# Batch 0's attention by halves of the heads, batch 1's turns by transfers, and batch 2's loads straight behind w_out

## The chip, the cores and the metric

The kernel runs on one core of one Trainium2 chip. The time is the device time of that core in microseconds (us), the median of several executions. The engines of the core work side by side and wait for one another by semaphores: TensorE (PE in the profile; its weight loads are the row PEld), VectorE (DVE), ScalarE (ACT) and GpSimd (POOL). SyncE (SP) only issues transfers. Transfers issued from SP and ACT go to queues that the profile names hardware_dynamic (q1 for SP), those from POOL to q0, software_dynamic. All of them are carried out by the same 16 DMA engines. GpSimd's queue can convert f32 to bf16 on the way.

## The reference

Two layers in a row: attention with a cosine weighting and no softmax, and a feed-forward layer with squared ReLU. There are 8 batches, 8 heads, 576 positions, 64 numbers per head; 4608 tokens of 512 numbers, and 2048 hidden units.

```python
r = np.maximum(x, 0.0)                              # for q and for k
phi = np.concatenate([r * c, r * s], axis=-1)       # c, s: cos and sin of the position
kv = np.einsum('bhsf,bhsd->bhfd', k_p, v)           # per head 128 x 64
z = np.sum(k_p, axis=2)                             # per head 128
num = np.einsum('bhsf,bhfd->bhsd', q_p, kv)
den = np.einsum('bhsf,bhf->bhs', q_p, z)[..., None] + 1e-06
x = (num / den)                                     # then tokens x (heads * 64)
h = x @ w_in
r = np.maximum(h, 0.0)
g = r * r
out = g @ w_out
```

## The kernel before, in words

**Tiling.** The 576 positions of a batch are four blocks of 128 (j = 0 to 3) and a tail of 64 (j = J = 4), which packs four heads over two halves of the partitions. Per block, `declare_feature` makes the cosine and the sine half of phi (a ReLU times a column, on ACT or DVE), `declare_v` casts v to bf16 beside a column of ones, and `declare_kz` multiplies k_p with v over the five blocks into two PSUM banks, so that kv and z come together. `declare_num` multiplies q_p with kv and z and then divides on DVE (three instructions), which gives x. Two turns (transposes) are needed: q_p must have its features on the partitions before `declare_num`, and x its channels before the feed-forward layer. There are two ways to turn: on PE through a matmul with the identity and a copy out of PSUM (`declare_qT_pe`, `declare_xT_pe`), or by a transposing transfer from SP (`declare_qT`, `declare_xT`). Before the change, batches 0 and 1 take the first, batches 2 to 7 the second.

**The feed-forward layer.** `declare_plain` makes one product of two blocks of hidden units with 256 tokens (8 matmuls into one bank), a ReLU on ACT into `rt` (two buffers), and a square on DVE into `gT`; a batch of 512 main tokens has 16 of them. The first two are split into pieces of 128 tokens. `declare_rows` multiplies batch 0's gT with w_out, 64 matmuls of 512 columns. Later batches use sums and differences of blocks of the weights (`declare_w1_sums`, `declare_w2_sums`, 7 products in place of 8). w_in and w_out come in four quarters each, cast to bf16 by GpSimd's queue: `load_w1(i, 4)`, `load_w2(i, 4)`. Product number hb needs quarter hb // 4.

**The order.** `prologue()` is written out by hand: the loads of batch 0, w_in, its attention up to x of blocks 0 and 1. The rest is declared as operations with their engines, costs, reads, writes and a place (`pos`), and `Planner.plan` puts them into an order by a list schedule: on PE by slot, on the other engines by how late an operation may be. `SHIFTS` lists corrections by number of operation (`n:by`, and an engine if one is fixed). `given` declares something that the prologue does, with the time at which the planner is to take it as done; `given([("w1", i)], ...)` does this for the quarters of w_in. The planner fixes the order of the instructions alone: each engine's queue then runs in that order, and waits are for data and buffers. In particular `pos` of a load holds nothing up on the chip. A POOL transfer also waits for the eighth POOL transfer before it, since eight semaphores go round.

**Buffers.** k, v and q have one f32 buffer each. So a load of the next batch waits until the engines have read the last piece of the one before. Six PSUM banks are free to all ("F"), two are for long sums ("B").

## Time and profile before

| what | us |
|---|---|
| median of 3 runs (lowest, highest) | 279.13 (278.8, 279.6) |
| the profiled execution | 278.33 |
| its span, first to last instruction | 276.6 |
| PE busy in the span | 269.0 |
| DVE, ACT, POOL busy | 219.1, 192.6, 28.4 |

The profiled execution is 1.7 us longer than its span. Its times count from the span's start. A row of the timeline gives the start, the time from there to the end of the last of the merged instructions, the engine, the line, the operation with out<-in, and in brackets the idle time ahead with what ended it. Most operations are issued by helpers, so one line (L429 is the helper of all matmuls, L418 the square, L407 and L405 the features) stands for many tiles, and the tiles tell them apart: `xT,w1sb` is a plain product, `w2sb,gT` of 512 columns are rows, `vx,kp` is kv and z, `kvz,sums` or `kvz,qpT` is the numerator, `ident,qp` (L580) and `ident,x` (L668) are turns on PE.

### The profile page before, as it was taken

Reading aid. Unit: us, or ns where it says so; the run is one execution under the profiler, and the core shown is the slowest. Engines: PE = TensorE matmul, PEld = TensorE weight load, DVE = VectorE, ACT = ScalarE, POOL = GpSimd, SP = SyncE. Lnnn points to the kernel's source line nnn. Section 1 sums busy time; section 2 is a strip of 40 time slices with the busy share of each in tenths; the row PEclk is TensorE's granted clock in tenths of the full one; section 3 lists DMA queues with packets and bytes.
Section 4 is the critical chain, followed back from the end, with each engine's and each line's share of the span. In section 5 each row is a group of like instructions: output and inputs, shape, how many; then the busy total and the mean of one; then the engine's idle time right before and its main releaser. Section 6 shows DMA issues by size and latency. Waiting matters only on the chain.

```text
span 276.6 us, 7125 instructions
## 1 busy us (share of the span) xinstructions
PE 269.0 (97%) x2846; PEld 227.8 (82%) x2851; DVE 219.1 (79%) x515; ACT 192.6 (70%) x385; POOL 28.4 (10%) x46
## 2 busy tenths in 40 slices
PE   8979999999999999999999999999999999999994
PEld 3658856789888988888888888988988888888883
DVE  1849996998795896799977999799946997279741
ACT  3767862798798796499848995699738643685421
POOL 8925244100000000000000000000000000000000
PEclk9999999999999999999999999999999999999999
DMA  7999999776999999899899428997583301200024
GB/s 228 311 206 287 330 256 374 220 174 148 368 191 257 281 248 238 220 331 160 237 266 377 114 40 167 330 219 210 57 233 77 94 32 42 112 1 2 8 88 134
DMA packets 77824, 53.01 MB, mean 192 GB/s; under 512 B 52032, under 2 KB 73024, under 8 KB 77792
## 3 DMA queue, kind: packets, MB, share of 16 engines
q1 hardware_dynamic: 70368, 37.63, 54.7%
q0 software_dynamic: 7280, 14.81, 19.8%
q8 instruction: 22, 0.36, 0.5%
q10 hardware_dynamic: 144, 0.13, 0.1%
q14 instruction: 10, 0.08, 0.1%
HBM read 36.70 MB, written 9.44 MB: 167 GB/s over the span
## 4 chain that ended last, share of the span: by engine, by line
PE 81%; DVE 11%; DMA 2%; issue 2%; POOL 2%; ACT 1%; POOLq 0%; DVEq 0%
PE banks L429 78%; DVE gT L418 3%; DVE rs L421 3%; DVE gs L426 3%; DMA q<-in_q_dram 2%; PE banks L580 1%; DVE gTt L418 1%; PE banks L668 1%; PE banks L1132 1%; ACT qp L405 1%; POOL kt L365 1%; DVE x L628 1%; POOL vt L365 0%; ACT sums L412 0%; DVE kp L407 0%
## 5 line engine op out<-in xcount | busy, mean ns | idle before, releaser
L429 PEld LDWEIGHTS <-w1sb 128*128 128x128 bf16 x784 | 72.7, 98 | 8.7
L429 PE MATMUL banks<-xT,w1sb 128*128 128x256 bf16 (+1 forms) x576 | 68.3, 267 | 0.1
L429 PEld LDWEIGHTS <-gs 128*128 128x128 bf16 x512 | 49.5, 98 | 7.0 <-DVE gs L426 0.7
L429 PE MATMUL banks<-w2sb,gT 128*128 128x256 bf16 (+1 forms) x284 | 44.8, 295 | 0.2 <-issue 0.2
L429 PEld LDWEIGHTS <-gT 128*128 128x128 bf16 x400 | 37.4, 98 | 7.5
L415 ACT ACTIVATE rt<-banks 128x512 bf16<-128x512 f32 x64 | 37.2, 602 | 9.2 <-PE banks L429 4.5
L429 PEld LDWEIGHTS <-w1s 128*128 128x128 bf16 x320 | 30.6, 98 | 3.9 <-issue 0.2
L429 PE MATMUL banks<-w2sb,gs 128*128 128x256 bf16 x256 | 32.7, 273 | 0.1
L429 PE MATMUL banks<-w2s,gs 128*128 128x256 bf16 x256 | 32.1, 273 | 0.1
L421 DVE CUSTOM_DVE_ANT_0 rs<-banks,sums 128x512 bf16<-128x512 f32 x40 | 27.0, 684 | 3.8 <-ACT sums L829 3.1
L418 DVE TENSOR_TENSOR gT<-rs 128x1024 bf16<-128x1024 bf16 (+1 forms) x50 | 28.0, 580 | 1.2 <-ACT rs L415 0.6
L426 DVE TENSOR_TENSOR ysb<-banks,sums 128x256 f32<-128x256 f32 x32 | 13.5, 422 | 17.6 <-PE banks L429 9.4
L418 DVE TENSOR_TENSOR gT<-rt 128x512 bf16<-128x512 bf16 x48 | 19.4, 420 | 7.1 <-ACT rt L415 7.0
L415 ACT ACTIVATE rs<-banks 128x512 bf16<-128x512 f32 x40 | 23.5, 606 | 2.0 <-PE banks L429 1.8
L405 ACT ACTIVATE kp<-k,sin_col 128x512 bf16<-128x512 f32 x32 | 22.4, 725 | 0.5 <-DMA k<-in_k_dram 0.5
L429 PE MATMUL banks<-xT,w1s 128*128 128x256 bf16 x160 | 22.7, 273 | 0.0
L429 PE MATMUL banks<-xs,w1s 128*128 128x256 bf16 x160 | 22.7, 273 | 0.0
L405 ACT ACTIVATE qp<-q,sin_col 128x512 bf16<-128x512 f32 x32 | 22.0, 720 | 1.0 <-DMA q<-in_q_dram 1.0
L426 DVE TENSOR_TENSOR gs<-gT 128x1024 bf16<-128x1024 bf16 x28 | 19.2, 689 | 3.1 <-PE banks L429 2.7
L628 DVE TENSOR_TENSOR x<-banks,den 128x512 bf16<-128x512 f32 x30 | 20.7, 691 | 1.0
L429 PE MATMUL banks<-xTt,w1sb 128*128 128x256 bf16 x128 | 16.1, 273 | 0.0
L407 DVE TENSOR_SCALAR kp<-k,cos_col 128x512 bf16<-128x512 f32 x26 | 12.0, 501 | 5.0 <-DMA k<-in_k_dram 5.0
(105 smaller groups left out, 362.8 us busy)
## 6 DMA issues: line engine op xcount, KB each, us to landing
out_dram<-ysb SPq DMA_DIRECT2D x13, 512.0 KB, 3.6
k<-in_k_dram SPq DMA_DIRECT2D x6, 1024.0 KB, 6.4
v<-in_v_dram SPq DMA_DIRECT2D x5, 1024.0 KB, 7.5
q<-in_q_dram SPq DMA_DIRECT2D x5, 1024.0 KB, 9.3
v<-in_v_dram POOLq DMA_DIRECT2D x3, 1024.0 KB, 8.2
w1sb<-in_moe_w_in_dram POOLq DMA_DIRECT2D x4, 512.0 KB, 10.9
w2sb<-in_moe_w_out_dram POOLq DMA_DIRECT2D x4, 512.0 KB, 12.4
q<-in_q_dram POOLq DMA_DIRECT2D x2, 1024.0 KB, 9.1
```

The lines of the kernel that those rows point to most:

```text
L365: eng.dma_start(out=tail[g * TAIL : (g + 1) * TAIL, :, :], in_=src[b, g * HH : (g + 1) * HH, MAIN:S, :].rearrange("h p d -> p h d"),)
L405: nc.scalar.activation(out=dst, in_=src, func=ACTF.Relu, scale=col)
L407: nc.vector.tensor_scalar(out=dst, in0=src, scalar1=0.0, scalar2=col, op0=ALU.max, op1=ALU.mult)
L415: nc.scalar.activation(out=out, in_=in_, func=ACTF.Relu)
L418: nc.vector.tensor_tensor(out=out, in0=in_, in1=in_, op=ALU.mult)
L421: nc.vector._custom_dve(TENSOR_ADD_SAT, out=out, in0=in0, in1=in1, s0=float("inf"), s1=0.0)
L426: nc.vector.tensor_tensor(out=out, in0=in0, in1=in1, op=op)
L429: nc.tensor.matmul(out=out, lhsT=lhsT, rhs=rhs, start=start, stop=stop, skip_group_check=True)
L580: nc.tensor.transpose(t[:, h, :], qp_at(b, j)[:, h, :], ident[:, :])
L628: nc.vector.tensor_tensor(out=x_at(b, j).rearrange("p (b k) (l d) -> p b k l d", b=n, l=2), in0=n4[:, :, :, 0:D].rearrange("p b (k l) d -> ...
L668: nc.tensor.transpose(t[:, kb, :], x_at(b, j)[:, kb, :], ident[:, :])
L1132: nc.tensor.matmul(out=banks[:, 6 + i % 2, :], lhsT=ident[:, :], rhs=zeros, start=True, stop=True)
```

## The change

It has four parts.

1. **Batch 0's attention.** It is no longer written out in the prologue but declared (`declare_first`) and ordered by the planner with everything else. All loads of batch 0 are issued by SP: k, k's tail, q's first half, v's tail, v in two halves of the heads, q's second half, q's tail. GpSimd makes the features of k's block 3. kv and z, the copy, the numerator, the division and the turn of x of blocks 0 and 1 are done for heads 0 to 3 first and then for heads 4 to 7. w_in's loads stand on POOL behind a one-element copy that reads v's first half. Between the planned operations of the head, `fill` puts matmuls without a use on PE where the planner sees a gap.
2. **Batch 1's turns.** `declare_att` now calls `declare_qT` and `declare_xT` for batch 1 as well: three transposing transfers for q_p, three for x.
3. **Order of the POOL transfers.** It becomes w_out's first quarter, q of batch 1, second quarter, k, v, third and fourth quarter, then q, k and v of batch 2. `declare_load` gets a parameter `gate` that could hold a load until some x has been made; no call gives it.
4. **The planner's figures.** Costs, `t0`, `T1` and all of `SHIFTS` are new.

```diff
-21:4.5 31:1.0 44:-3.0 53:1.5 60:1.0 74:3.0 80:2.0 93:-7.5 105:-0.5 132:-2.5 134:2.0 146:-7.0
...
+10:-5.0 29:-12.0 33:-3.0 37:-2.5 43:-9.5:ACT 48:2.5 73:-1.5 77:-3.5 90:-21.0:ACT 109:0.5 111:5.5
...
-    def declare_load(b, nm, eng, pos=None, after=()):
+    def declare_load(b, nm, eng, pos=None, after=(), size=3.4, gate=None):
...
+                if gate and fn is load_main:
+                    nc.gpsimd.tensor_copy(out=at(buf)[0:1, 0, 0, 0:1], in_=x_at(*gate)[0:1, 0, 0:1])
                 fn(src, nm, buf.i, b, queue)
...
-            if b > 1 and (j == J or j % 2):
+            if j == J or j % 2:
                 declare_qT(b, j // 2)
-            elif b == 1:
-                declare_qT_pe(b, j, npos[j] - 3.5, DVE1)
         for j in range(NS):
             declare_num(b, j, npos[j])
-            if b > 1 and (j == J or j % 2):
+            if j == J or j % 2:
                 declare_xT(b, j // 2)
-            elif b == 1:
-                declare_xT_pe(b, j, npos[j] + 2.0, BOTH)
...
     def prologue():
+        for src, nm, part in (
+            (k, "k", 0), (k, "kt", 0), (q, "q", 0), (v, "vt", 0), (v, "v", 0), (v, "v", 1), (q, "q", 1), (q, "qt", 0)
+        ):
...
-        load_main(k, "k", 0, 0, nc.sync)
-        load_tail(k, "k", 0, 0, nc.gpsimd)
-        load_main(v, "v", 0, 0, nc.gpsimd)
-        load_tail(v, "v", 0, 0, nc.gpsimd)
         constants()
-        load_main(q, "q", 0, 0, nc.gpsimd, 2)
-        for i in range(31):
-            nc.tensor.matmul(out=banks[:, i % 2, :], lhsT=zeros[:, 0:P], rhs=zeros, start=True, stop=True)
...
+        fill(28)
+        for c, col in ((0, cos_col), (D, sin_col)):
+            nc.gpsimd.tensor_scalar(
+                out=at(kp_of(0, J - 1))[:, :, c : c + D], in0=piece("k", 0, J - 1),
+                scalar1=0.0, scalar2=col[:, J - 1 : J], op0=ALU.max, op1=ALU.mult,
+            )
+        nc.gpsimd.tensor_copy(out=w1sb[0:1, 0, 0:1], in_=mem["v"][0:1, 0, 0, 0, 0:1])
         for i in range(4):
             load_w1(i, 4)
...
+    def fill(n):
+        for _ in range(n):
+            nc.tensor.matmul(out=banks[:, SPARE, :], lhsT=zeros[:, 0:P], rhs=zeros, start=True, stop=True)
...
     for i in range(4):
-        given([("w1", i)], 12.2, size=2.6)
+        given([("w1", i)], 11.7, size=2.6)
...
+    def declare_first():
+        feature = lambda nm, j, c: declare_feature(nm, 0, j, c, BOTH)
...
+        for g in range(2):
+            hs = slice(g * HH, (g + 1) * HH)
...
+            for j in (J, *range(J)):
+
+                def kz(_, j=j, g=g):
...
+        for g in range(2):
+            den, bks = plan.buf("den"), [plan.buf("F"), plan.buf("F")]
+            for j in range(2):
+
+                def num(_, j=j, g=g, bk=bks[j]):
...
+    ORDER1 = []
+    pos = 21.0
+    for nm in "0q1kv23----QK-V":
+        if nm != "-":
+            ORDER1.append((pos, nm))
+        pos += 1.0 if nm == "-" else 2.65 if nm in "0123" else 3.1
...
-    declare_load(1, "q", "POOL", 17.0)
-    declare_w2_load(0, 19.0, 10.0)
-    declare_load(1, "k", "POOL", 20.0)
-    declare_w2_load(1, 22.0, 11.0)
-    declare_load(1, "v", "POOL", 23.0)
-    declare_w2_load(2, 25.0, 12.0)
-    declare_w2_load(3, 26.0, 13.0)
-    declare_att(1, T2[0] + 4.5, [T2[0] + x for x in (6.0, 9.0, 12.0, 14.0, 19.0)], DVE1, DVE1, DVE1)
-    for nm in "qkv":
-        declare_load(2, nm, "POOL", 28.0)
+    declare_transfers([x for x in ORDER1 if not x[1].isupper()])
+    declare_att(1, T2[0] + 4.5, [T2[0] + 6.5 + 1.0 * x for x in range(NS)], DVE1, DVE1, DVE1)
+    declare_transfers([x for x in ORDER1 if x[1].isupper()])
...
-    t0 = {"PE": 16.8, "ACT": 17.3, "DVE": 17.1, "SP": 10.0, "POOL": 20.0, "GIVEN": 0.0}
+    t0 = {"PE": 8.0, "ACT": 6.3, "DVE": 6.3, "SP": 10.0, "POOL": 14.2, "GIVEN": 0.0}
...
+            if op.eng == "PE" and op.start < SPARE_UNTIL:
+                if end:
+                    fill(int((op.start - end - 0.2) / 0.22))
+                end = op.end
             op.fn(op.eng)
```

Built, the changed program has these differences in order that the diff doesn't show by itself. On PE, 31 matmuls of `fill` stand in the head. Behind the four split pieces on w_in's first quarter come 16 matmuls on the third quarter, and only then 16 on the second: among the operations that `SHIFTS` counts, number 10 is now the `given` of the third quarter, while the loads themselves keep the order 0, 1, 2, 3. Then come 56 matmuls of products, the turn of q's tail, 16 more, the tail's numerator, 4 of the rows, the last product, the turn of x's tail, and the rest of the rows with batch 1's kv and numerators in between: 22 rows, kv and z (with 2 and 4 rows), both numerators on the first transfer of q_p, 10 rows, one numerator on the second transfer, 2 rows, one numerator, 6 rows, the tail's numerator, 14 rows; and then batch 1's products. On DVE the first sum of w_in's blocks stands in front of block 2's division and also reads the third quarter. On POOL, batch 2's v stands behind batch 0's first store of rows, which waits for ACT's copies of the finished rows.

## The prediction

> **What bounds the kernel now.** I read the page's busy times first, then the slices, the windows of the first 60 us, the timelines of PE, DVE and POOL there, and the transfers.
>
> ```profile
> PE 269.0 (97%) x2846; PEld 227.8 (82%) x2851; DVE 219.1 (79%) x515; ACT 192.6 (70%) x385; POOL 28.4 (10%) x46
> ...
> PE   8979999999999999999999999999999999999994
> ...
> q1 hardware_dynamic: 70368, 37.63, 54.7%
> q0 software_dynamic: 7280, 14.81, 19.8%
> ```
>
> PE is the bound from 18.5 us to the end, so a microsecond saved on PE or in the head counts in full, and so does each one for which PE waits. The queue lines also give mean sizes: 37.63 MB / 70368 = 535 B a packet on q1, 2034 B on q0. The windows (columns PE, PEld, DVE, ACT, POOL, clock, DMA share, GB/s) show a second full resource:
>
> ```profile
> 15.00:20.00 5.00, 3.70 (x49) 2.63 (x48) 2.00 (x6) 3.71 (x6) 1.12 (x2) 1.00 1.24 206
> 25.00:30.00 5.00, 4.97 (x50) 4.36 (x49) 4.97 (x16) 3.68 (x7) 2.06 (x4) 1.00 1.05 394
> 35.00:40.00 5.00, 5.00 (x35) 2.90 (x34) 5.00 (x14) 4.11 (x8) 2.76 (x4) 1.00 1.17 251
> 45.00:50.00 5.00, 4.97 (x52) 3.12 (x52) 3.94 (x11) 2.18 (x4) 1.79 (x4) 1.00 1.02 372
> 54.00:55.00 1.00, 1.00 (x22) 1.00 (x19) 0.96 (x3) 1.00 (x3) 0.00 (x0) 1.00 1.15 212
> ```
>
> The DMA engines are full from 5 to 50 us, DVE from 25 to 40. The last row is a transposing transfer of q_p alone: 512 KB at 212 GB/s, 2.5 us of all 16 engines. PE's timeline shows the work that the change touches:
>
> ```profile
> 18.49 1.50 PE L429 MATMUL banks<-xT,w1sb 128*128 128x128 bf16 x24
> ...
> 25.34 0.39 PE L580 MATMUL banks<-ident,qpt 128*128 128x128 bf16 x4
> 25.56 6.28 PE L429 MATMUL banks<-xT,w1sb 128*128 128x256 bf16 x56
> ...
> 37.35 0.61 PE L580 MATMUL banks<-ident,qp 128*128 128x128 bf16 x8
> 37.80 2.97 PE L429 MATMUL banks<-w2sb,gT 128*128 128x512 bf16 x13
> ...
> 68.32 1.13 PE L429 MATMUL banks<-vx,kp 128*128 128x65 bf16 x32
> ```
>
> Start to start, eight turns cost 0.45 us, four 0.22. Batch 1's products end at 68.32. POOL's timeline tells when quarters of w_in land, as POOL waits for them:
>
> ```profile
> 21.71 0.90 POOL L357 DMA_DIRECT2D v<-in_v_dram  x1 [0.29 <-DMA w1sb<-in_moe_w_in_dram]
> 24.24 1.25 POOL L365 DMA_DIRECT2D kt<-in_k_dram  x2 [1.63 <-DMA w1sb<-in_moe_w_in_dram]
> ```
>
> The third quarter is there at 21.7, the fourth at 24.2. The same bytes (k, v, q, then w_in) stand ahead of them afterwards, through engines that are full from 5 us, so I keep these times.
>
> **What the Trainium skill says.** "DMA: Bandwidth & Descriptors", section "Queues, rings and completion order": every DMA engine serves all queues and takes turns between them packet by packet. The trace before never has transposes beside a full q0 for long, so the share that they get isn't shown. The same page, "Latency and other measured facts", gives 261 GB/s for a transposing transfer; the trace says 212, and I use that. "TensorE: Matmul & The Clock Gate", section "What's actually happening": about 3.4 us of idle time halves PE's clock, and about as much work restores it. The clock is 1.00 in all windows here; the first fillers, 0.43 us apart up to 7.1 us and 0.21 after, agree with a start at half rate.
>
> **Part by part.** All sums are against the profiled execution (span 276.6, 1.7 around it); I add the difference to the median, 279.13, since 278.33 is 0.8 below it.
>
> *Turns of batch 1 off PE.* q_p: 4 x 0.45 + 0.22; x: 4 x 0.22 + 0.11. That is 3.0 us of PE, on the path. Their copies (0.60 us each for q_p on DVE, 0.5 for x) were beside PE's work; I count nothing.
>
> *The head.* Half heads let x come sooner: v's second half about 11.5, cast, kv, copy, numerator, two divisions and a turn of about 4.5 together, so about 16, where the first product could start; 18.49 is now. But the gain isn't kept. The four split pieces end near 19.2, and the next products need the third quarter, at 21.7, because the order on PE takes it before the second. PE waits 2.5 us. From 21.7: two products 1.75, numerator and turn 0.47, two products 1.75, turn 0.22: the run of 56 starts at 25.9. Now the same work is done at 25.34. The head loses 0.55 us in place of gaining 2. If the third quarter came 0.7 earlier or later, so would this. The 2.5 us are under the 3.4 of the clock gate. GpSimd's two features are hidden: kv needs v anyway, and w_in's loads wait for v's first half as well.
>
> *From there without waits.* 9 products 7.86, tail turn 0.22, last product 0.87, turn of x's tail 0.11, 64 rows at 0.2155 = 13.8, kv and z 1.2, the numerators 4 x 0.245 + 2 x 0.25: 25.5 us. Batch 1's products could start at S = 51.4, and take 32 x 0.0556 + 112 x 0.1092 = 14.0. They would end at 65.4, 2.9 before 68.32. So the difference is S - 54.3, and S is what has to be found. Later work is the same on PE, which is full there: the difference is carried to the end.
>
> *When the transfers of q_p start.* q of batch 1 lands at 29.4 as before (w_out's first quarter ahead of it in both). Its cosine features stand on DVE behind 2 sums of w_in's blocks that also wait for 21.7, two divisions of 1.05, 26 squares and sums, and a copy. Start to start those take 0.336 us:
>
> ```profile
> 28.92 0.42 DVE L418 TENSOR_TENSOR gT<-rt 128x512 bf16<-128x512 bf16 x1
> 29.26 0.42 DVE L426 TENSOR_TENSOR w1s<-w1sb 128x512 bf16<-128x512 bf16 x1
> ```
>
> 21.7 + 0.67 + 2.1 + 8.7 + 0.3 + two features 0.8 = 34.3; the first transfer is issued at 34.5 and moves at 35.9 (the first one now: issued 52.17, moving from about 53.5). DVE goes on to batch 1's k and v: the last cast near 42.1, kv done 42.3, the first numerator possible at 43.2.
>
> *What the DMA engines have at 35.9.* On q0, by the landings of before (w_out's last quarter: issued at 32.24, 11.0 to landing, so 43.2), the rest of v and its tail, and two quarters of w_out: 7.4 us. Behind them, no longer held back by anything but buffers, q of batch 2, issued about 39, and k, about 41: 6 us with tails. On q1, 2.5 + 2.5 + 0.65 = 5.65 us of transposes. PE needs the first transfer at 43.2, w_out's third quarter at 43.7, the second transfer 2.2 us later, the fourth quarter at 47. All of it together can't be done before 35.9 + 13.05 = 48.95. The share of the transposes decides. Taken as 0.5: third quarter at 35.9 + 4.95 / 0.5 = 45.8, S = 53.6. Taken as 0.7: v late, S = 54.3. Taken as 0.36: first transfer 43.4, in time; second at 35.9 + 5 / 0.36 = 49.8 plus 0.6 to land, while PE stands ready at 46.1; then 22 rows and three numerators, 5.45: S = 55.9. Taken as 0.12: below. I take 0.36, a value between the ends: a transposed packet has 256 B, one of q0 1 to 4 KB, which speaks for a small share; that transposes may go several to a turn speaks against a very small one. S = 55.9 is +1.6.
>
> *Other edits.* x's transfers (1.25 us each) come behind q_p's and beside batch 2's k; the first is issued near 46 and lands by 53, before S; if it were delayed too, 1 us per us. Batch 2's v waits behind the store of rows and lands near S + 10, when its casts are due: nothing if so, else 1 to 2 us. ACT has the 16 ReLUs of batch 1 (8.3 us) with batch 2's features (5.8) and copies (2.6) in one stretch, 16.7 us against 16 of PE: 0 to 1 us, I take 0. The new numbers in the list of shifts can make or remove small waits later: windows from 65 to 260 show 0.2 us of idle PE, so nothing to win, and I take 0 (-0.3 to +1).
>
> **Forecast**, chance 0.36: PE waits about 2.5 us for w_in and about 4.4 for q_p's second transfer; 279.13 + 1.6 = 280.7, of its own range 279.9 to 283.5.
>
> **Rival 1, faster**, 0.26: transposes and loads overlap in the DMA engines, since they read SBUF and HBM; S is 51.6, 276.4. For it: the share of 1.24 with w_in says that packets of one engine overlap. Against: 212 GB/s while transposing alone, at 1.15. It decides when the second transfer lands before 47 and w_out's last quarter before 47.5.
>
> **Rival 2, the loads crowd the transposes out**, 0.20: one packet each in turn. In 2.5 us an engine does 2048 / 16 = 128 packets of a transfer, 20 ns each; q0's take 98 ns (window with w_out: 789 packets in 4 us on 16 engines at 1.196) to 164. Some 115 packets of q0 are left at 35.9 up to batch 2's k; they need 13.4 us and let 115 of 128 pass. The first transfer lands near 52.4; PE waits 9 us; S = 61, +6.7: 285.8, and up to 1.7 more for the clock.
>
> **Rival 3, no change**, 0.18: a share of 0.5 to 0.7, where the sum of the DMA work alone binds; S = 53.6 to 54.3: 278.4 to 279.1.
>
> **How the numbers follow.** A difference of 0.3% (0.84 us) is about what a measurement of this kernel can tell. Faster: rival 1 with a little of rival 3, 0.28. Same: the rest of rival 3 and the forecast's lower edge, 0.15. Slower: 0.57. The range, 276.3 to 287.0, holds rivals 1 and 2 but for the latter's clock loss.
>
> **What would show it.** Right: PE idle from about 19 to 21.7, its wait ended by a transfer of w1sb; the run of 56 products near 25.9; no L580 or L668 for qp and x of batch 1; PE idle between 43 and 51 in front of `kvz,qpT`; DMA share above 1 until 50; batch 1's products from near 56. Wrong: that run before 25, `qpT` transfers that land within 6 us of issue, or PE full from 22 to 52 (rival 1); a first `qpT` that lands after 50 (rival 2); or a wait behind 66 us, which none of the cases has.

## The result, and the profile after

The changed kernel takes 297.74 us (median of 293.54, 295.02, 300.46 and 303.92), the kernel before 279.37 in the same comparison. The ratio is 1.053, with a 95% interval of 1.0462 to 1.0599; it is taken from 293.54 and 295.02 alone, since the two runs above 300 lie more than 1.5% above the fastest and count as slow. The forecast of 280.7 and its range up to 287.0 are both too low.

The profiled execution took 295.02 us, its span is 293.2: 16.6 more than the 276.6 of before. The page's busy times, slices and queues after:

```profile
PE 267.1 (91%) x2785; PEld 226.0 (77%) x2789; DVE 216.3 (74%) x507; ACT 192.3 (66%) x387; POOL 26.4 (9%) x40
...
PE   8878992099999799999999999999999999999992
...
q1 hardware_dynamic: 82240, 41.89, 61.5%
q0 software_dynamic: 6528, 12.32, 17.3%
```

PE is busy 1.9 us less (269.0 to 267.1): the turns of batch 1 have left it. But it stands idle for 26.1 us where it was 7.6: 18.5 more, less the 1.9, makes the 16.6. The slices with 2 and 0 (44 to 58.6 us) show where. PE's waits name the transfers (columns: who waited for whom, total us, times, longest). `qpT` is q_p turned, `xT` is x turned, `w1sb` is w_in:

```profile
PE banks L430 <- DMA qpT<-qp: 12.8, 1, 12.8
PE banks L430 <- DMA xT<-x: 1.9, 1, 1.9
PE banks L430 <- DMA w1sb<-in_moe_w_in_dram: 1.9, 2, 1.4
```

One wait is most of the loss. PE's timeline (L430 is now the helper of matmuls) gives the steps that the prediction numbered:

```profile
17.32 1.75 PE L430 MATMUL banks<-xT,w1sb 128*128 128x128 bf16 x16 [0.50 <-DMA w1sb<-in_moe_w_in_dram]
...
22.95 1.92 PE L430 MATMUL banks<-xT,w1sb 128*128 128x256 bf16 x16 [1.37 <-DMA w1sb<-in_moe_w_in_dram]
...
28.84 5.40 PE L430 MATMUL banks<-xT,w1sb 128*128 128x256 bf16 x48 [0.41 <-ACT xT L413]
...
58.60 1.06 PE L430 MATMUL banks<-kvz,qpT 128*128 128x65 bf16 x16 [12.81 <-DMA qpT<-qp]
59.48 3.49 PE L430 MATMUL banks<-w2sb,gT 128*128 128x512 bf16 x10
...
68.40 14.18 PE L430 MATMUL banks<-xT,w1sb 128*128 128x256 bf16 x144
```

The first products on the third quarter wait until 22.95. The last of the big run, which began at 27.40 and goes on at 28.84, ends at 34.24; the run of before ended at 31.84, so the head is 2.4 us later, not 0.55. Then PE stops at 45.8 for 12.81 us in front of batch 1's first numerators, and when it goes on its clock is slow: ten rows take 3.49 us, 16 small matmuls 1.06. Batch 1's products start at S = 68.40; S = 54.3 would have meant no change, so this is 14.1 of the 16.6. The 1.9 us for a transfer of x come at 100.06, in front of batch 2's products on turned x.

The third quarter of w_in came later because its loads were issued later. POOL's timeline has this, first before, then after:

```profile
7.96 3.29 POOL L372 DMA_DIRECT2D w1sb<-in_moe_w_in_dram  x4
```

```profile
11.54 3.21 POOL L373 DMA_DIRECT2D w1sb<-in_moe_w_in_dram  x4 [0.31 <-POOL w1sb L1083]
```

The windows (columns PE, PEld, DVE, ACT, POOL, clock, DMA share, GB/s) that answer to those of before:

```profile
15.00:20.00 5.00, 3.86 (x39) 3.40 (x40) 2.19 (x9) 2.22 (x6) 2.87 (x5) 0.75 1.23 203
35.00:40.00 5.00, 4.95 (x42) 3.15 (x41) 4.93 (x15) 4.92 (x10) 0.85 (x2) 1.00 1.07 326
45.00:50.00 5.00, 0.80 (x3) 0.18 (x2) 0.00 (x0) 0.46 (x1) 0.00 (x0) 0.82 1.08 268
50.00:55.00 5.00, 0.00 (x0) 0.00 (x0) 0.00 (x0) 0.00 (x0) 0.00 (x0) 0.50 1.14 237
55.00:60.00 5.00, 1.40 (x18) 1.12 (x19) 0.67 (x3) 0.00 (x0) 0.00 (x0) 0.50 1.37 151
```

From 46 to 58 no engine works and the DMA engines are full: the kernel waits for them alone. The clock falls to 0.50 in the long wait. It is 0.75 already at 15 to 20, because it was 0.50 from 17.48 to 20.90. In the 3.41 us ahead of that PE was busy for 2.09 us, and none of its waits was longer than 0.5 us.

SP's queue shows the two transposing transfers of q_p, 22.09 us in its queue where two of them (batch 2's) took 7.78 before. They were issued at 36.12 and 44.7, with 22.4 and 15.5 us to landing (58.5 and 60.2); before, a pair had 4.4 and 4.9. First before, then after:

```profile
52.17 7.78 SPq L567 DMA_TRANSPOSE qpT<-qp  x2
```

```profile
36.12 22.09 SPq L575 DMA_TRANSPOSE qpT<-qp  x2
```

What went through the DMA engines meanwhile can be counted from the trace's packets. The table gives packets per microsecond that were under way on each queue, and the share of the 16 engines' time (shares of overlapping packets can sum to more than 1). q1 has 256-byte packets of q_p and hardly anything else; q0 has 1 KB at first, 4 KB later.

```
us      q0 packets  q0 share    q1 packets  q1 share
36-40   114 to 218  1.02-1.22        0        0
42         167        0.91         155       0.32
45          93        0.78         221       0.36
47          74        0.96          59       0.07
48          90        0.95          79       0.11
49         105        0.94          95       0.10
50          99        0.88          87       0.10
51          28        0.93          15       0.18
52         109        0.86         150       0.22
55          28        0.18         221       1.31
57           7        0.05         171       1.35
59           0        0           1136       1.25
```

Three things are in it. The first packet of a transpose moves at 40.24, 4.1 us after issue; before it was 1.3 (52.17 to 53.45). At 41 to 43 (packets of 1 KB on q0) and at 46 to 50 (4 KB for the most part) the queues go about one packet for one packet, whatever the size: at 49 that is 352 GB/s for q0 and 23 for the transposes. It isn't a strict rule: at 45 and 52 more transposed packets pass than packets of q0, at 51 fewer. And from 54 to 58, with q0 nearly empty, the transposes still run at a fifth of the rate of 59 or less; at 56 and 57 half of their packets take 171 ns or more, where 18 ns is usual at 49 and at 59.

### The profile page after: what moved, and what is told of

Its sections match the earlier page's. It is cut to its first block, busy times and chain, and to the rows that moved or that the text cites. A ratio compares the mean times of both kernels' runs of the same rounds, so it can differ in the third digit from the quotient of the medians.

```text
span 293.2 us, 7015 instructions
## 1 busy us (share of the span) xinstructions
PE 267.1 (91%) x2785; PEld 226.0 (77%) x2789; DVE 216.3 (74%) x507; ACT 192.3 (66%) x387; POOL 26.4 (9%) x40
## 4 chain that ended last, share of the span: by engine, by line
PE 73%; DMA 16%; DVE 5%; POOL 2%; ACT 2%; issue 1%; DVEq 0%; ACTq 0%; POOLq 0%
PE banks L430 73%; DMA qpT<-qp 8%; DMA w1sb<-in_moe_w_in_dram 3%; DMA xT<-x 3%; DMA k<-in_k_dram 2%; POOL kp L1079 2%; DVE gs L427 1%; DVE gT L419 1%; ACT rt L416 1%; DVE rs L422 1%; POOL w1sb L373 1%; DVE x L636 0%; DVE gTt L419 0%; ACT qp L406 0%; ACT rs L416 0%
## 5 line engine op out<-in xcount | busy, mean ns | idle before, releaser
L430 PEld LDWEIGHTS <-w1sb 128*128 128x128 bf16 x784 | 74.1, 99 | 13.3 <-issue 3.2
L430 PE MATMUL banks<-xT,w1sb 128*128 128x256 bf16 (+1 forms) x576 | 69.3, 271 | 4.2 <-DMA xT<-x 1.9
L430 PEld LDWEIGHTS <-gs 128*128 128x128 bf16 x512 | 49.3, 98 | 6.5 <-issue 0.3
L416 ACT ACTIVATE rt<-banks 128x512 bf16<-128x512 f32 x64 | 37.8, 600 | 13.5 <-PE banks L430 7.8
L430 PEld LDWEIGHTS <-gT 128*128 128x128 bf16 x400 | 38.1, 98 | 10.4 <-issue 1.6
L430 PE MATMUL banks<-w2sb,gT 128*128 128x256 bf16 (+1 forms) x285 | 45.0, 301 | 0.3 <-issue 0.2
L430 PEld LDWEIGHTS <-w1s 128*128 128x128 bf16 x320 | 30.7, 98 | 3.5
L430 PE MATMUL banks<-w2sb,gs 128*128 128x256 bf16 x256 | 32.4, 273 | 0.1
L430 PE MATMUL banks<-w2s,gs 128*128 128x256 bf16 x256 | 32.4, 273 | 0.0
L416 ACT ACTIVATE rs<-banks 128x512 bf16<-128x512 f32 x40 | 22.7, 602 | 2.1 <-PE banks L430 1.9
L634 DVE TENSOR_SCALAR den<-banks 128x8 f32<-128x8 f32 (+1 forms) x38 | 6.1, 159 | 23.3 <-PE banks L430 23.2
L430 PE MATMUL banks<-xs,w1s 128*128 128x256 bf16 x160 | 23.0, 273 | 0.0
L430 PE MATMUL banks<-kvz,qpT 128*128 128x65 bf16 x224 | 11.2, 197 | 12.8 <-DMA qpT<-qp 12.8
L430 PE MATMUL banks<-xT,w1s 128*128 128x256 bf16 x160 | 22.7, 273 | 0.0
L430 PEld LDWEIGHTS <-qpT 128*128 128x128 bf16 x224 | 10.3, 99 | 14.3 <-DMA qpT<-qp 13.3
```

What stands on the lines that cost most here:

```text
L416: nc.scalar.activation(out=out, in_=in_, func=ACTF.Relu)
L430: nc.tensor.matmul(out=out, lhsT=lhsT, rhs=rhs, start=start, stop=stop, skip_group_check=True)
L634: nc.vector.tensor_single_scalar(out=d, in_=n4[:, :, :, D], scalar=EPS, op=ALU.add)
```

## The experiments

Each ratio is to the kernel before, measured at the same time. All but `head` and its relatives, `part2` and the two probes start from the changed kernel.

### Which part loses: part2, head, pe_turns

`part2` is the kernel before with batch 1's turns by transfers. Its numerators are placed as in the changed kernel, and its list of shifts is kept on the same operations; the rest is as before.

```diff
-            if b > 1 and (j == J or j % 2):
+            if j == J or j % 2:
                 declare_qT(b, j // 2)
-            elif b == 1:
-                declare_qT_pe(b, j, npos[j] - 3.5, DVE1)
...
-            if b > 1 and (j == J or j % 2):
+            if j == J or j % 2:
                 declare_xT(b, j // 2)
-            elif b == 1:
-                declare_xT_pe(b, j, npos[j] + 2.0, BOTH)
...
-    declare_att(1, T2[0] + 4.5, [T2[0] + x for x in (6.0, 9.0, 12.0, 14.0, 19.0)], DVE1, DVE1, DVE1)
+    declare_att(1, T2[0] + 4.5, [T2[0] + 6.5 + 1.0 * x for x in range(NS)], DVE1, DVE1, DVE1)
```

> Part 2 alone: before, with batch 1's q_p and x turned by transfers and its numerators placed as after; head, order of the POOL transfers and shifts are those of before (on the same operations). Batch 2's loads are held there by nothing but buffers, too. If the transposes and the loads beside them are the cause, it is slow without the other parts: the first q_p transfer lands behind 48, PE waits 4 us or more for it, 285 to 292. If the new order of the loads (part 3) or the head is needed for that, 279 to 281.

Measured: 304.12 us, ratio 1.0922 [1.0862, 1.0983]. PE's timeline of `part2`:

```profile
64.71 1.06 PE L439 MATMUL banks<-kvz,qpT 128*128 128x65 bf16 x16 [20.31 <-DMA qpT<-qp]
```

The transfers were issued at 33.25 and 40.3 and landed at 51.5 and 64.7; PE stood still until the second: in this kernel its first numerator reads the second transfer (the instruction waits for that transfer's semaphore), where the changed kernel has both numerators on the first transfer in front. So this part alone, with w_out and batch 2's loads in their old order, is enough for the loss, and for more than the loss of all parts together; PE's order is likely a part of that surplus. From 45 to 49 us both queues crawled here (52 to 60 GB/s for the two together, and a packet of q0 took 0.5 to 0.8 us in the mean); that stretch I can't explain.

`head` is the other way round: the halves of the heads alone, with turns, loads, planner's costs and shifts (moved by 58 numbers) of before.

```diff
-            if j == J or j % 2:
+            if b > 1 and (j == J or j % 2):
                 declare_qT(b, j // 2)
+            elif b == 1:
+                declare_qT_pe(b, j, npos[j] - 3.5, DVE1)
...
-    declare_transfers([x for x in ORDER1 if not x[1].isupper()])
+    declare_load(1, "q", "POOL", 17.0)
+    declare_w2_load(0, 19.0, 10.0)
...
-10:-5.0 29:-12.0 33:-3.0 37:-2.5 43:-9.5:ACT 48:2.5 73:-1.5 77:-3.5 90:-21.0:ACT 109:0.5 111:5.5
...
+79:4.5 89:1.0 102:-3.0 111:1.5 118:1.0 132:3.0 138:2.0 151:-7.5 163:-0.5 190:-2.5 192:2.0 204:-7.0
```

> Part 1 alone: the new head of batch 0 in front of everything else as before (turns on PE, the old order of the POOL transfers, the old shifts on the same operations); the quarters of w_in are loaded and taken in the order 0, 1, 2, 3. PE starts its products near 17.4 in place of 18.49, but w_in's quarters land 1.4 later than before, as GpSimd's two features of 2.25 us stand in front of their issue: the last near 25.7 in place of 24.2. So the first 12 products end near 32.2 in place of 31.84, and the time is 279 to 280: half heads win nothing because w_in sets the pace. If the head of after is bad by itself (theory C), 281.5 or more.

Measured: 282.16, ratio 1.0092 [1.0063, 1.0121]. Here PE takes the quarters of w_in in their order, and yet the first twelve products end at 34.26, 2.4 us after those of before. Waits of 1.01 us (ending at 21.57) and 0.46 (at 26.66) for w_in are in it, though the first products start at 18.17, 0.3 before the old ones. POOL's timeline of `head` says why: w_in is issued from 12.21, where it was 7.96.

```profile
8.51 2.14 POOL L1072 TENSOR_SCALAR kp<-k,sin_col 128x512 bf16<-128x512 f32 x1
11.46 0.44 POOL L1076 CAST w1sb<-v 1x1 bf16<-1x1 f32 x1 [0.81 <-DMA v<-in_v_dram]
12.21 3.26 POOL L362 DMA_DIRECT2D w1sb<-in_moe_w_in_dram  x4 [0.31 <-POOL w1sb L1076]
```

Batches 2 to 4 are 2.2 us late too (the last part of their kv and z, the tail's, starts at 71.58, 93.44, 108.31 against 69.39, 91.25, 106.12), later ones 3.8 to 3.9. So the halves start the first products sooner and cost some 2.2 us in the head all the same, and about 1.6 arise later, in an order of operations that isn't fitted to this mix.

`pe_turns` is the changed kernel with batch 1's turns back on PE and its numerators at their old places (the same edit of `declare_att` as in `head`), its loads as changed.

> After, but with batch 1's q_p and x turned on PE again, placed as before, and the list of shifts kept on the same operations; batch 2's loads are not held. Theory A: without transposes the loads of batch 2 harm nothing, and what is left is the head's loss of about 2.2 us (run of 56 products at 27.4 and a 0.4 us wait in it, against 25.34): 281.3. Theory C, a good part of the loss is in the new order of the later work: 285 or more.

Measured: 287.17, ratio 1.0295 [1.0254, 1.0336]. The changed kernel's ratio is 1.053: with the turns on PE again 0.0235 of the loss of 0.053, a little under half, is gone. PE's timeline:

```profile
23.23 3.17 PE L440 MATMUL banks<-xT,w1sb 128*128 128x256 bf16 x16 [3.11 <-DMA w1sb<-in_moe_w_in_dram]
```

The wait for the third quarter is longer here (3.11) and the clock drops: 16 matmuls take 3.17 us where 1.92 is usual, and the windows 20 to 25 and 25 to 30 show 0.87 and 0.79. About 3.6 us more are idle after 85, in waits for ACT and DVE, and the shifts weren't fitted to the kernel with turns on PE; so 287.17 isn't a clean price of the rest.

### How the queues share: small, hold_q, hold_x, hold_q_w1, alone, probe, probe2

`small` loads q of batch 2 in four pieces instead of one, to make its packets smaller.

```diff
-                fn(src, nm, buf.i, b, queue)
+                if (b, nm) == (2, "q") and fn is load_main:
+                    fn(src, nm, buf.i, b, queue, [slice(i, i + 1) for i in range(J)])
+                else:
+                    fn(src, nm, buf.i, b, queue)
```

> After, but with q of batch 2 loaded in four pieces of one block each, so that the same bytes come in smaller and four times as many packets (the trace is to show the size). Theory A says that turns are taken per packet: the first q_p transfer then passes while q comes, and lands near 51 to 52; the second has k of batch 2 in large packets beside it and lands near 57 to 58; products of batch 1 start near 62 to 64, about 290. If the engines shared by bytes or by queue time, or if the transposes are slow by themselves (B), nothing changes: 58.5, 68.4, 295.

Measured: 302.07, ratio 1.083 [1.0781, 1.0879]. The packets stayed at 4096 bytes, so this tells nothing of their size. But the first transfer landed later still:

```profile
63.45 1.06 PE L430 MATMUL banks<-kvz,qpT 128*128 128x65 bf16 x16 [16.69 <-DMA qpT<-qp]
```

And it shows the slow tail for longer: from 55 to 63 us q0 has 35% of the engines' time, then down to 9%, in 9 to 34 packets a microsecond, while the transposes run at 22 to 47 GB/s with 103 to 213 packets. One for one no longer explains that: q0 leaves most of the engines' time free.

`hold_q` makes batch 2's loads wait for q_p's second transfer, through a one-element copy on POOL ahead of them.

```diff
+                if (b, nm) == (2, "q") and fn is load_main:
+                    nc.gpsimd.tensor_copy(out=at(buf)[0:1, 0, 0, 0:1], in_=at(qpTb[1, 1])[0:1, 0, 0:1])
                 fn(src, nm, buf.i, b, queue)
```

> After, but with batch 2's load of q (and what stands behind it on POOL: k and v of batch 2) held by a one-element copy that reads q_p's second transfer. Theory A, batch 2's loads crowd out the transposes packet for packet: after w_out's last quarters have passed at 45 about 1000 of the first transfer's 2048 packets are left, which take 1.3 us alone; it lands near 46.7 in place of 58.5, the second near 49.3 in place of 60.2, batch 1's products start near 55 in place of 68.4, and the time is near 281.6. Theory B, these transfers are slow by themselves (they began to move 4 us after their issue, and were slow at 54 to 58 with hardly anything on q0): the first still lands behind 54, the products start behind 63, 290 or more.

Measured: 296.98, in runs from 289.95 to 299.66; the spread is too wide for a ratio, and I use the trace alone (execution 289.95). Its transfer was issued at 37.80 and landed at 49.9:

```profile
49.91 0.66 PE L430 MATMUL banks<-kvz,qpT 128*128 128x65 bf16 x16 [2.46 <-DMA qpT<-qp]
...
59.85 14.18 PE L430 MATMUL banks<-xT,w1sb 128*128 128x256 bf16 x144
```

S falls from 68.40 to 59.85. So batch 2's loads cost 8.6 us at S in this pair of traces, more than theory B allowed and less than theory A had; beside w_out and the rest of batch 1's loads, which this run doesn't hold, the transfer still takes 12.1 us.

`hold_x` does the same with x's second transfer as the signal, and issues batch 2's loads behind it.

```diff
+                if (b, nm) == (2, "q") and fn is load_main:
+                    nc.gpsimd.tensor_copy(out=at(buf)[0:1, 0, 0, 0:1], in_=at(xT_of(1, 1))[0:1, 0, 0:1])
                 fn(src, nm, buf.i, b, queue)
...
+            if op.n in (198, 200, 201):
+                late.append(op)
+                continue
             op.fn(op.eng)
+            if op is turned["x", 1, 1]:
+                for o in late:
+                    o.fn(o.eng)
```

> After, but with batch 2's loads held until x's second transfer of batch 1 has landed. Theory A: as with the hold on q_p (products of batch 1 from 55), with x's transfers also alone; the loads of batch 2 begin near 54, k lands near 62, and kv of batch 2 is due near 70, so 281.6 again, or up to 2 more if batch 2's v comes late. Theory B: 290 or more.

Measured: 293.09, ratio 1.0506 [1.0472, 1.0541]. S is 61.04, 7.4 earlier than in the changed kernel, but the ratio is hardly better (1.0506 against 1.053). Batch 2's q is issued at 61.68, not 40.39; ACT waits 7.7 us for q over the kernel (2.8 in the changed one), with features that stand ahead of ReLUs of batch 1's products in its order, and PE waits for these:

```profile
50.35 1.06 PE L430 MATMUL banks<-kvz,qpT 128*128 128x65 bf16 x16 [4.04 <-DMA qpT<-qp]
...
70.16 3.00 PE L430 MATMUL banks<-xT,w1sb 128*128 128x256 bf16 x24 [1.93 <-ACT rt L416]
```

`hold_q_w1` is `hold_q` with the order of w_in's loads of `w1order` (below).

> After, with w_in's quarters in the order 0, 2, 1, 3 and batch 2's loads held behind q_p's second transfer. Theory A: q_p's first transfer is issued near 34.5, begins to move some 4 us later as in the other runs, shares with w_out's last quarters to about 44.5 and lands near 47.5 (49.7 with the hold alone); products of batch 1 start near 57.5 and the time is near 287. If w_out's quarters are what sets the landing, as they are issued by POOL and don't depend on the head, it lands near 49 and nothing is gained on the hold alone: 289.5.

Measured: 296.48, ratio 1.0574 [1.0489, 1.0658]. q_p was issued at 34.46 and landed at 50.5, for the most part beside 1-KB packets of w_out alone (42 to 46 us: some 150 packets of each queue per microsecond, one for one again). Then batch 2's q, released by that landing, ran into x's transfers:

```profile
67.11 9.25 PE L430 MATMUL banks<-xT,w1sb 128*128 128x256 bf16 x80 [6.35 <-DMA xT<-x]
```

A good part of the wait has moved from q_p's transfers (5.89 us are left) to x's. `alone` asks what is left if q_p has the engines to itself: `w1order`, and w_out's third and fourth quarters wait for q_p's second transfer.

```diff
+        def load(_):
+            if i == 2:
+                nc.gpsimd.tensor_copy(out=w2sb[0:1, 2 * HB // 4, 0:1], in_=at(qpTb[1, 1])[0:1, 0, 0:1])
+            load_w2(i, 4)
```

> After with w_in's quarters in the order 0, 2, 1, 3, and with w_out's third quarter (and so everything behind it on POOL) held until q_p's second transfer has landed, so that q_p's transposes have only the end of batch 1's v beside them. Theory A (one q0 packet against one packet of the transposes, and all engines in step with the one that has most of q0 left): with nothing on q0 from 38.5 the first transfer lands near 41, the second near 44 (50.5 and 52 with w_out's quarters beside them). PE then waits for w_out's third quarter, near 48, and x's transfers meet batch 2's q as before, so the time need not fall: 285 to 293. Theory B (the transposes are slow by themselves behind a q0 that has been busy): the first lands behind 46.

Measured: 289.57, ratio 1.0388 [1.034, 1.0436]. q_p was issued at 33.70, its transfers landed by 43.0 and at 46.2, and at 42 to 44 they ran at 283 to 290 GB/s. The numerators didn't wait; the rows did:

```profile
43.60 0.65 PE L430 MATMUL banks<-kvz,qpT 128*128 128x65 bf16 x16
53.70 4.27 PE L430 MATMUL banks<-w2sb,gT 128*128 128x512 bf16 x10 [9.45 <-DMA w2sb<-in_moe_w_out_dram]
```

So crowding is what makes q_p late: with q0 nearly empty from 39 on the first transfer took 9.3 us to land in place of 22.4. Holding w_out for that makes w_out late. No run has an order in which neither waits, and none shows that there is one.

The probes put known loads beside transposes late in the kernel before, where little else is under way. `probe` loads 1 MB on q0, into a buffer free by then, beside batch 6's transfers, and two small loads beside batch 7's; `probe2`, whose edit is shown, has 16 loads of 64 KB, eight packets of 8 KB each, beside batch 7's.

```diff
+            if (b, i) == (7, 0):
+                rows = k[0].rearrange("h s d -> (h s) d")
+                free = mem["k"][:, 0].rearrange("p h j d -> p (h j d)")
+                for m in range(16):
+                    p0, p1 = (8 * m, 8 * m + 8) if b == 7 else (0, P)
...
+                    nc.gpsimd.dma_start(
+                        out=free[p0:p1, :],
+                        in_=rows[p0 * 32 : p1 * 32].rearrange("(p j) d -> p (j d)", j=32),
+                    )
             nc.sync.dma_start_transpose(out=at(dst), in_=s)
```

> Before, with loads that nothing reads put on POOL's queue beside q_p's transposes of batch 6 (1 MB, all partitions) and batch 7 (2 x 64 KB, 8 partitions each), where the transposes are alone in before: two transfers in 5.0 us, some 800 to 1000 packets in a microsecond. If turns are taken packet for packet, the 1 MB lets few transposes pass while it runs (80 to 150 in a microsecond, as in after) and delays them by 2.5 us or more. If all engines keep step with the slowest, the 128 KB, should they fall to a few engines, hold the transposes of all engines at 100 to 250 packets in a microsecond for as long as they run; if they are spread evenly, they run for less than 0.5 us and nothing is seen. If the slow stretches in after (40 GB/s with hardly anything on q0) have another cause, the 128 KB do nothing although the trace shows them on few engines (share of q0 under 0.2).

> Before, with 16 loads of 64 KB (8 partitions each) that nothing reads on POOL's queue beside q_p's transposes of batch 7. The last probe showed such a load as 8 packets of 8192 B of some 0.5 us, so half of the engines or fewer are busy with it, and q0's share was 0.2 to 0.36; but it was over before the transposes began. If all engines keep step with the slowest, the transposes of all engines pass at 200 packets in a microsecond or fewer while these loads run, with most of the engines free; if each engine goes on by itself, the free half passes 400 or more.

Measured: 284.87 and 286.72, one execution each; only their traces are used. In `probe`, at 172 to 175, 16, 21, 45 and 33 packets of q0 started per microsecond and 41, 0, 26 and 32 of the transposes: about one for one at 8 KB too (115 to 99 in all), and 1058 per microsecond when q0 was empty. The small loads of batch 7 were done before the transposes began and tell nothing. For `probe2` the table counts the 8-KB packets of q0 and the 256-byte packets of the transposes that start in each microsecond:

```
us      q0 started  q0 share    q1 started  q1 share
206         10        0.50         156       0.63
207         11        0.53          19       0.74
208         11        0.53           0       0.81
209          8        0.50           0       0.85
210          0        0.41          49       0.95
212          0        0            975       1.30
213          0        0           1053       1.27
```

About eight of these packets of q0 are under way at once, nine at most, each for 0.92 us, so they have about half of the engines' time. If each engine went its own way, the other half would pass transposes at some 500 a microsecond, by an estimate from the 1053 at 213. But from 207.4 to 210.7 not one starts or ends. Thirteen stand open all that time, and for 4.8 us each in all: the 0.8 of q1's share are packets that wait. The same happens from 198.9 to 200.2, with eleven.

So packets of q0 that take up only a part of the engines can stop a whole transposing transfer. That is a likely cause of the slow tails of the changed kernel and of `small`, where q0 is nearly empty and the transposed packets are slow on all engines; it isn't shown for them. Nor does it give a rate. One transposed packet per packet of q0, on all 16 engines in step, would be 17 per microsecond here (16 in 0.92 us), and none passed. And the engines aren't strictly in step: from 210.7 to 212.1 some 270 other packets went by while the thirteen stood open. In `small` the trace has the 16 landing signals of the first transfer between 60.2 and 63.4. What holds the engines up, no trace shows.

`warm` asks what the lost clock costs: `w1order` with 55 matmuls without a use in front of the numerators, to keep PE warm through the wait.

```diff
             kvz, t = at(kvzb[b]), at(qT)
+            for _ in range(55 if (b, j) == (1, 0) else 0):
+                nc.tensor.matmul(out=bank(bks[0]), lhsT=w2sb[:, 0, 0:P], rhs=w2sb[:, 1, :], start=True, stop=True)
```

> After with w_in's quarters in the order 0, 2, 1, 3, and with 55 matmuls without a use (512 columns each, some 11.9 us) in front of batch 1's first numerators, where PE waits 12 us in the same kernel without them. Their results are overwritten. If the slow matmuls behind that wait (10 rows in 4.46 us in place of 2.17) come from PE's clock, they run at full rate now, batch 1's products start near 64.2 in place of 67.14 with the transfers landing at the same time, and the time is 2.5 to 3 below: 289.5. If they wait for data, nothing changes: 292.4.

Measured: 292.56, ratio 1.0471 [1.041, 1.0532], the same as `w1order`. PE's timelines, first of `w1order`, then of `warm`:

```profile
56.32 1.06 PE L430 MATMUL banks<-kvz,qpT 128*128 128x65 bf16 x16 [12.00 <-DMA qpT<-qp]
57.19 4.46 PE L430 MATMUL banks<-w2sb,gT 128*128 128x512 bf16 x10
```

```profile
57.13 2.32 PE L430 MATMUL banks<-w2sb,gT 128*128 128x512 bf16 x10
...
97.26 4.53 PE L430 MATMUL banks<-xT,w1sb 128*128 128x256 bf16 x40 [2.11 <-DMA xT<-x]
```

Ten rows take 2.32 us in place of 4.46, and S is 64.88 against 67.14: in `w1order` the clock costs 2.3 us at that place. But the time doesn't move: batch 2's products on turned x begin at 97.26, where `w1order` has 97.78, since PE now waits longer for that x (2.11 us against 0.86) and for a q_p (0.31).

### The head: w1order, pe_w1, and five forms of the halves

`w1order` loads the quarters in the order in which PE takes them.

```diff
-        for i in range(4):
+        for i in (0, 2, 1, 3):
             load_w1(i, 4)
```

> After, with w_in's quarters loaded in the order 0, 2, 1, 3 in which PE and DVE take them. The wait of PE for w_in near 21 goes; the first 12 products end near 31.4 in place of 34.2. Theory A (batch 1's start is set by q_p's transfers beside batch 2's loads, not by PE): the transfers are issued up to 2 us earlier but still land behind the loads, near 57; at most 2 of the 2.8 us arrive in the time: 293 to 295. The other theory, that the head's loss is carried to the end: 292.2.

Measured: 292.4, ratio 1.0448 [1.0375, 1.052], where the changed kernel has 1.053. The run of 56 starts at 25.86 and ends at 32.15 (34.24 in the changed kernel), while the stall at q_p stays at 12.00 us. `pe_w1` joins it with `pe_turns`.

> After with batch 1's turns on PE and w_in's quarters in the order 0, 2, 1, 3. With the turns on PE the PE sequence is nowhere held by transposes, so what the early third quarter costs must show in full: the wait of 3.1 us near 20 shrinks to 0.6, and PE's matmuls behind it (16 products in 3.17 us in place of 1.91) are at full rate: 3.5 to 4 us less than 287.2, 283.2 to 283.7. If it is carried only in part, 284.5 to 286.

Measured: 284.06, ratio 1.0204 [1.0166, 1.0243]: 3.1 us below `pe_turns` in the medians, 0.0091 or 2.5 us in the ratios. So taking the third quarter before the second costs 2.5 to 3 us where nothing hides it.

The rest start from `head`. `head_nopool` takes the two features of k's block 3 from GpSimd; DVE and ACT make them.

```diff
-        for c, col in ((0, cos_col), (D, sin_col)):
-            nc.gpsimd.tensor_scalar(
...
-                if j == J - 1:
-                    given([(kp_of(0, j), j % 2, c)], 7.6 if c == "c" else 8.9, lat=0.0)
-                else:
-                    feature("k", j, c)
+                feature("k", j, c)
```

> As part 1 alone, but with the features of k's block 3 on DVE and ACT in place of GpSimd, so that w_in's loads are issued as soon as v's first half is there. If GpSimd's features delay w_in, the last quarter lands near 24.2 again, the first 12 products end near 31.3, and the time is 0.5 to 1 below the head with GpSimd: 278 to 279. If they are hidden, as the prediction had it, the two are the same.

Measured: 281.78, ratio 1.0081 [1.0059, 1.0104], as `head`. POOL's timeline:

```profile
11.38 0.44 POOL L1071 CAST w1sb<-v 1x1 bf16<-1x1 f32 x1 [9.51 <-DMA v<-in_v_dram]
```

Without the features POOL waits 9.51 us and lets w_in go at 12.12 instead of 12.21: the features are hidden, and v's first half is what holds w_in. `head_gate_q` lets the one-element copy read q's first half instead, and `head_nopool_gate_q` does both.

```diff
-        nc.gpsimd.tensor_copy(out=w1sb[0:1, 0, 0:1], in_=mem["v"][0:1, 0, 0, 0, 0:1])
+        nc.gpsimd.tensor_copy(out=w1sb[0:1, 0, 0:1], in_=mem["q"][0:1, 0, 0, 0, 0:1])
```

> Part 1 alone, but with the copy that holds w_in's loads reading q's first half in place of v's first half, which lands some 3 us earlier. If that copy is what makes w_in late (issued at 12.2 in place of 7.96 before, last quarter 1.4 us later), the last quarter lands near 24.5, the 16 products of batch 0 come 1 to 1.5 us earlier and the time is 280.7 to 281.2, against 282.2 for part 1 alone. If the engines are full anyway and v only comes later for it, it stays at 282 or above.

> Part 1 alone with both edits that each changed nothing: k's block 3 off GpSimd, and w_in's loads held by q's first half in place of v's. GpSimd's features end at 10.6 and v's first half lands at 11.4, so each may have covered the other; without both, w_in's loads are issued near 9. If their late issue is what makes the head lose, the last quarter of w_in lands a microsecond or more sooner and the time falls by 1 us or more from 282.2, to 281 or less. If the engines are full in any case, it stays within 0.5 of 282.

Measured: 282.21, ratio 1.0137 [1.0065, 1.021], and 285.88, ratio 1.0243 [1.0172, 1.0315]. In the first, w_in goes at 11.06 and PE waits 1.63 us for it at 19.09, more than in `head`. In the second it goes at 8.83, and now q's tail, which SP's queue brings last, is late: its features, on ACT 3.90 us idle until 19.92 and on DVE until 19.93, stand ahead of the copy of x, and PE waits 4.23 us for that at 21.38. Letting w_in in sooner goes with late loads on the other queue; holding it makes it late itself.

`head_fifo` therefore puts q, v and w_in one behind the other on POOL's queue and the tails of k and v on SP's; `head_one_queue`, whose edit is shown, puts these tails there too. Neither has the one-element copy or features on GpSimd.

```diff
-        for src, nm, part in (
-            (k, "k", 0), (k, "kt", 0), (q, "q", 0), (v, "vt", 0), (v, "v", 0), (v, "v", 1), (q, "q", 1), (q, "qt", 0)
-        ):
...
+        load_main(k, "k", 0, 0, nc.sync)
+        load_tail(k, "k", 0, 0, nc.gpsimd)
+        load_main(q, "q", 0, 0, nc.gpsimd, half(0))
...
+        load_main(q, "q", 0, 0, nc.gpsimd, half(1))
         for i in range(4):
             load_w1(i, 4)
+        load_tail(q, "q", 0, 0, nc.gpsimd)
```

> Part 1 alone with k's block 3 off GpSimd, and with batch 0's q and v and w_in all on POOL's queue one behind the other, as before (k and two tails stay on SP), without the copy that holds w_in. Theory: the head loses because its loads stand on two queues: held, w_in is issued at 12.2 and the engines are idle in part at 12 to 14; not held, w_in and q share packet for packet and q is late (the run before). In one queue nothing is held and nothing shared: w_in is issued near 8, its last quarter lands near 24.2 as before, PE starts its products near 17.3, the first 12 products end near 31.2 (31.84 before, 34.26 for part 1 alone), and the time is 278 to 279.5, 3 us under part 1 alone. If the half heads themselves are the loss, it stays near 282.

> As the run before (head_fifo), but with the tails of k and v also on POOL's queue, in the places that they have in the order of part 1; only k's main blocks stay on SP. In the run before, these two tails stood on SP beside a full POOL queue and landed at 8.5 and 11.9, so kv came 3 us late, although w_in was in time. If that was all, the tails land near 4 and 8, PE starts its products near 17.5, the first 12 products end near 31.3 and the time is 278 to 279.5. If the half heads themselves lose, it stays near 282.

Measured: 282.54, ratio 1.0118 [1.0074, 1.0163], and 282.28, ratio 1.0123 [1.009, 1.0157]. In `head_fifo` the two small tails, alone on the second queue beside full transfers, came so late (k's landed at 8.5, v's at 11.8) that DVE waited 1.58 us for k's and 1.70 for v's, and the first products started at 20.42. In `head_one_queue` they came in time (6.7 and 8.2) and the numerator of q's tail starts at 32.75, against 34.20 in `head`, 33.85 in `head_nopool` and 31.77 before: of the 2.4 us lost in the head 1.4 are back when the loads stand in one queue, without the copy and without GpSimd's features. But the end doesn't follow. Batches 2 and 3 are 0.9 us late and batch 7 3.7 (its tail's kv and z at 204.42 against 200.73), by small waits (0.40 at 100.40, 0.35 at 162.80) and a different order. What makes these in the later batches stays open. None of the kernels is faster than the one before.

## Why the prediction was wrong

**PE's turns: right.** 3.0 us of turns were to leave PE, and they did. Busy time fell by 1.9 only; the slower clock of 17 to 21 and 48 to 62 us made other work longer, which fits the difference.

**The head: the place right, two terms missed.** PE does take the third quarter first and waits for it at the place named. "So I keep these times" failed: the same bytes stood ahead of w_in, but its issue moved from 7.96 to 11.54, since the copy that holds it waits for POOL's features and v's first half. The quarter came at 22.9 and not 21.7. The clock was the other: the prediction set a wait of 2.5 us against 3.4 us of idle time and kept the full clock. No wait there reached 2.5 us, and the clock was 0.50 from 17.48 to 20.90 all the same. The term of 0.55 measured 2.4; `pe_w1` against `pe_turns` prices the order of the quarters at 2.5 to 3.1.

**GpSimd's features: right in effect** (`head` and `head_nopool` agree), and so is the reason, v's first half. What I didn't ask is what that half holds back.

**The share of the transposes: the step that failed.** I chose 0.36, between ends, on the ground that several transposed packets might go in one turn. With it the first transfer was to land at 43.4, in time, and the second to cost 4.4 us. The first landed at 58.5 and cost 12.81: 18.3 us after its first packet, for what is 2.5 us of work alone, so its share was about 0.14. The Trainium skill, "DMA: Bandwidth & Descriptors", section "Queues, rings and completion order", which the prediction named, says that each engine takes turns packet by packet; a packet there is several descriptors, so it leaves open how many of the 256-byte packets that the trace counts go in one turn. At 46 to 50 us about one did (105 of q0 to 95, 90 to 79), at 45 more (93 to 221), and in `probe2` none for 3.3 us. This was near to rival 2, at 0.20.

**Rival 2's own sum was too small as well.** It had the first transfer landing at 52.4; it was 58.5. Of these 6.1 us, 1.6 are the later issue (36.12 for 34.5), 2.7 the first packet's start (4.1 us after issue with a full q0, as against 1.4). The rest, 1.8, the sum had no term for. It let each engine pass its 128 packets by itself, and it has no slow tail: from 54 to 58 hardly anything of q0 was left, and the transposes crawled. `probe2` makes it likely, but doesn't show, that the last packets of q0, on few engines at a time, held up all of them. Strictly in step they weren't: by 58.5, 2791 transposed packets had started, 743 more than the first transfer has. From that landing to S the sum had 8.6 us; it was 9.9, and the clock accounts for the 1.3 (ten rows in 3.49 us, where `warm` has 2.32), within the 1.7 that rival 2 allowed. 6.1 and 1.3 make S 68.4 for 61.

**x's transfers and batch 2.** "1 us per us" was the right warning, but in the changed kernel PE lost nothing to batch 1's x; the 1.9 us at 100.06 are batch 2's. In `hold_q_w1` batch 1's x did cost 6.35 and 3.36 us. And each way of helping q_p that was tried passes the wait on: to x (`hold_q_w1`), to batch 2's features (`hold_x`), to w_out (`alone`). The prediction's own count, that all of it can't be done before 48.95 when PE needs the first piece at 43.2, was a reason to doubt any forecast below S = 54.3; I spread the chances as if only a share were unknown.

**The direction** was right, and so was the stall in front of `kvz,qpT`, from 45.8; but it was the first transfer that PE waited for, not the second. The sign "a wait behind 66 us, which none of the cases has" did come.

**Open.** What holds the transposes up from 54 to 58; the stretches in which both queues crawl (51 in the changed kernel, 45 to 49 in `part2`); how much of `part2`'s surplus PE's order explains; and 1.6 to 2.8 us in later batches with the halves alone. No run has the new order of POOL's transfers or the planner's new figures alone.

## What to carry to other kernels

A transposing transfer on one queue beside a full queue of large packets shouldn't be costed at its rate alone. Here about one 256-byte packet passed for each packet of 1 to 8 KB over most stretches, and at times none: 13 to 23 GB/s (46 to 51 us) and 22 us to landing, against 212 GB/s and 4.4 us when the other queue is empty. Taking 3 us off the bound engine by giving work to the DMA engines pays only in a stretch in which they have room; ask first what they must bring in that stretch, and by when. And a load that is held behind a signal is to be followed to its own reader: its lateness comes back there.

## What the runs showed of the hardware that was not expected

- With half of the DMA engines' time free and at most nine 8-KB packets under way, a transposing transfer stood still for 3.3 us (`probe2`, 207.4 to 210.7) with 13 of its packets open, each for 4.8 us; without them it started 975 to 1053 packets a microsecond.
- The first packet of a transposing transfer moved 4.0 to 4.4 us after issue beside a full q0 (4.1 in the changed kernel, 4.4 in `w1order`, 4.0 in `hold_q`), and 1.3 us with q0 nearly empty (before).
- Transposes alone ran at up to 290 GB/s (`alone`, 43 to 44 us), above the 212 that the prediction took from a window of before.
- The tails of k and v, two loads of 64 KB each, on a second queue beside full transfers landed 1.8 and 3.6 us later than with all loads in one queue (`head_fifo` against `head_one_queue`): not only transposes can come late there.
- PE's clock was 0.50 for 3.4 us in the head of the changed kernel (17.48 to 20.90), behind 3.41 us in which PE was busy for 2.09 and had no wait longer than 0.5 us.
